# Two half-height passes in place of two full ones at the end of each projection

## The chip, the cores and the metric

The kernel runs on one core of a Trainium2 chip. The metric is the device time of one execution in microseconds (us). The kernel before has a median of 625.88 us over three runs (625.6 to 626.61). Engine names are those of the profile: PE is TensorE doing matmuls, PEld is TensorE loading the stationary operand ("weight load"), DVE is VectorE, ACT is ScalarE, POOL is GpSimd, SP is the queue that issues the transfers.

## The reference

Two linear-attention blocks read the same x (2048 rows of 576 numbers, 32 heads of 18) and are mixed by a gate that is computed from x:

```python
qkv = x @ wqkv                                  # A and B have weights of their own
# A: phi(t) = where(t > 0, t + 1, exp(t)) + 1e-6
# B: phi(t) = [softmax(t @ w_phi), softmax(-(t @ w_phi))]
kv  = einsum("bhsd,bhse->bhde", phi(k), v);  z = phi(k).sum(over s)
o   = einsum("bhqd,bhde->bhqe", phi(q), kv) / (einsum("bhqd,bhd->bhq", phi(q), z) + 1e-6)
a, b = oA @ woA, oB @ woB
g   = sigmoid((x * gate_w).sum(-1))
out = g * a + (1 - g) * b
```

All arrays are float32.

## The kernel before

**Tiles.** x is cut into 16 tiles of 128 rows and arrives transposed, so that the 576 columns of x lie on the partitions: four k-tiles of 128 rows, and a fifth (index 4) for the 64 that are left, which the host stores twice, in rows 0 to 63 and again in rows 64 to 127.

**Split operands.** The matmuls run on a rounded type, so each operand is kept as a high part and the rest: `load_x` makes `xh` and `xl`, `load_w` (through `split`) and `fold_w` make a weight tile `W` with nine slots: slots 0 to 3 are the high parts of k-tiles 0 to 3, slots 5 to 8 their low parts. Slot 4 is the tail: since the tail's rows stand twice, it holds the high part in rows 0 to 63 and the low part in rows 64 to 127.

**A projection** is x times one weight matrix, 576 columns (578 with the gate's two), in two column halves of `HB` = 288, each into a PSUM bank of its own. `proj` does one half in 14 passes of TensorE: for each of the four full k-tiles high x high, high x low, low x high; then `xh` with slot 4, which does the tail's high x high and high x low in one pass; then `xl` with slot 4. In this last pass only rows 0 to 63 give something that is wanted (low x high); rows 64 to 127 multiply low by low. There are 6 weight matrices and 16 tiles of x, so 96 projections and 192 halves: 2688 passes, all on line 157.

**The stages.** In the first, `do_v` makes the values (two halves, each in a one-bank PSUM tile `tr`, of which there are two), `do_ak` and `do_bk` the keys (`do_pq`: one two-bank tile `pq`, of which there are two), and `kv_a` and `kv_b` (line 212) add a tile's products to two PSUM banks `bk` that stay open for the whole stage. These last matmuls have 57 or 38 columns of stationary operand and write to PSUM partitions from 0 or from 64 on, in turn. Between the stages the sums are folded into the output weights; there line 351 writes 64 PSUM partitions at a time in the same manner. In the second stage `q_units` makes the queries of one tile (projections with `WBq` and `WAq`, into `pq`), `tr_units` transposes the features of the tile before, `num` and `out_units` finish an earlier one.

**Order.** The order of each engine's instructions is fixed when the program is built: a list scheduler follows the order of the code, the buffers and its own timing model, and may put matmuls of one group between those of another.

Of the kernel before, what the change touches and what calls it, by code (L numbers as in the profile page):

```python
# [10 lines left out]
AF = mybir.ActivationFunctionType  # L11
ALU = mybir.AluOpType
AX = mybir.AxisListType

P = 128
S, D, H, DH = 2048, 576, 32, 18
NT = S // P
KT = 5
HB = 288
# [9 lines left out]
def tile_gated_mix(ctx, tc, xT, wAk, wAv, wBv, wAq, wkT, wqT, phi, woA, woB, out):  # L29
    nc = tc.nc  # L30
    V, A, G, PE = nc.vector, nc.scalar, nc.gpsimd, nc.tensor
# [7 lines left out]
    def r(ap):  # L39
        return ap.bitcast(F32)  # L40

    def pq_tile():
        return ps.tile([P, 2, 512], F32, name="pq")

    def tr_tile():
        return ps.tile([P, 512], F32, name="tr")
# [4 lines left out]
    def row_tile():  # L51
        return wk.tile([P, 640], F32, name="row", bufs=6)

    def wraw_tile():
        return wk.tile([P, 640], F32, name="wraw", bufs=3)

    def uw_tile():
        return wk.tile([P, 2, D], F32, name="uw", bufs=3)
# [39 lines left out]
    def load_x(t, eng=G):  # L98
        raw = wk.tile([P, 640], F32, name="xraw")
        nc.sync.dma_start(raw, xT[t].rearrange("p j n -> p (j n)"))  # L100
        raw = raw.rearrange("p (j n) -> p j n", n=P)
        xh = wk.tile([P, KT, P], F32R, name="xh")
        xl = wk.tile([P, KT, P], F32R, name="xl")
        A.activation(xh, raw, AF.Copy)  # L104
        eng.tensor_tensor(xl, raw, r(xh), op=ALU.subtract)  # L105
        return xh, xl


    def w_tile():
        return wp.tile([P, 9, 578], F32R, name="W")  # L110

    def split(src, hi, lo, eng=V, raw=None):
        raw = (wraw_tile() if raw is None else raw)[:src.shape[0], :src.shape[1]]
        nc.sync.dma_start(raw, src)
        A.activation(hi, raw, AF.Copy)  # L115
        a = P - lo.shape[0] if hi.shape[0] == P else 0
        eng.tensor_tensor(lo, raw[a:], r(hi[a:]), op=ALU.subtract)

    def load_w(src, n, eng=V, raws=(None,) * KT):
        W = w_tile()  # L120
        for j in range(4):
            split(src[:, j, :], W[:, j, :n], W[:, 5 + j, :n], eng, raws[j])
        split(src[:, 4, :], W[:, 4, :n], W[64:, 4, :n], eng, raws[4])
        return W

    def fold_w(src):
        W = w_tile()
        ph = row_tile()
        nc.sync.dma_start(ph[:126, :630], phi)
        for g, nh in GROUPS:  # L130
            n = nh * DH
            c = slice(126 * g, 126 * g + n)
            raw = wraw_tile()
            nc.sync.dma_start(raw[:n, :], src[:n, g, :])
            if g % 2:
                p1, p2 = tr_tile(), tr_tile()
            else:
                pq = pq_tile()
                p1, p2 = pq[:, 0], pq[:, 1]
            for i in range(KT):  # L140
                dst = p1[:, 126 * i:126 * i + n] if i < 4 else p2[:, :n]
                PE.matmul(dst, raw[:n, P * i:P * i + P], ph[:n, 126 * g:126 * g + n], start=True, stop=True)  # L142
            p1v = p1[:, :504].rearrange("p (i c) -> p i c", c=126)[:, :, :n]
            A.activation(W[:, 0:4, c], p1v, AF.Copy)
            A.activation(W[:, 4, c], p2[:, :n], AF.Copy)
            V.tensor_tensor(W[:, 5:9, c], p1v, r(W[:, 0:4, c]), op=ALU.subtract)
            V.tensor_tensor(W[64:, 4, c], p2[64:, :n], r(W[64:, 4, c]), op=ALU.subtract)
        return W

    def proj(dst, x, W, c0, n):  # L150
        xh, xl = x
        steps = []
        for j in range(4):
            steps += [(xh, j, j), (xh, j, 5 + j), (xl, j, j)]
        steps += [(xh, 4, 4), (xl, 4, 4)]
        for i, (xx, j, w) in enumerate(steps):
            PE.matmul(dst, xx[:, j, :], W[:, w, c0:c0 + n], start=(i == 0), stop=(i == len(steps) - 1))  # L157

    def halves(p):
        return p[:, :, :HB]  # L160
# [1 line left out]
    def heads(p):  # L162
        return p[:, :, :HB].rearrange("p a (h d) -> p a h d", d=DH)

    def bc2(t):
        return t.rearrange("p (a h) -> p a h", a=2)[:, :, :, None].to_broadcast([P, 2, 16, DH])


    def phi_elu(pq):
        f = row_tile()  # L170
        fx = f[:, :D]
        fv = fx.rearrange("p (a b) -> p a b", a=2)
        A.activation(fv, halves(pq), AF.Exp)  # L173
        V.tensor_scalar(fx, fx, 1.0, EPS, op0=ALU.min, op1=ALU.add)  # L174
        V.scalar_tensor_tensor(fv, halves(pq), 1.0 + EPS, fv, op0=ALU.add, op1=ALU.max)  # L175
        return f

    def softmax_exp(pq):
        mm = sm.tile([P, 64], F32, name="mm")
        V.tensor_reduce(mm[:, :32], heads(pq), op=ALU.max, axis=AX.X)  # L180
        V.tensor_reduce(mm[:, 32:], heads(pq), op=ALU.min, axis=AX.X)
        uw = uw_tile()

        def v4(s):
            return uw[:, s, :].rearrange("p (a h d) -> p a h d", a=2, d=DH)

        V.tensor_tensor(v4(0), heads(pq), bc2(mm[:, :32]), op=ALU.subtract)
        V.tensor_tensor(v4(1), bc2(mm[:, 32:]), heads(pq), op=ALU.subtract)  # L188
        A.activation(uw, uw, AF.Exp)  # L189
        ss = sm.tile([P, 64], F32, name="ss")  # L190
        V.tensor_reduce(ss, uw.rearrange("p s (h d) -> p (s h) d", d=DH), op=ALU.add, axis=AX.X)  # L191
        rs = sm.tile([P, 64], F32, name="rs")
        V.reciprocal(rs, ss)  # L193
        return uw, rs
# [32 lines left out]
                     uw[:, :, 54 * gr:54 * gr + DH * nh], p == 1)  # L227

    def do_v(t, x, W, which):
        for hf in range(2):  # L230
            pv = tr_tile()
            proj(pv[:, :HB], x, W, HB * hf, HB)
            A.activation(vt[t % 2][:, which, 16 * hf:16 * hf + 16, :DH],  # L233
                         pv[:, :HB].rearrange("p (h d) -> p h d", d=DH), AF.Copy)

    def do_pq(x, W, n=D):
        pq = pq_tile()
        proj(pq[:, 0, :HB], x, W, 0, HB)
        proj(pq[:, 1, :n - HB], x, W, HB, n - HB)
        return pq  # L240

    def do_ak(x):
        return phi_elu(do_pq(x, WAk))
# [6 lines left out]
    xs = {0: load_x(0, V)}  # L250
    spare = [u[:, i] for u in (uw_tile(), uw_tile(), uw_tile()) for i in range(2)]
    WAv = load_w(wAv, D, raws=[None, None, None] + spare[:2])
    xs[1] = load_x(1)
    do_v(0, xs[0], WAv, 0)
    do_v(1, xs[1], WAv, 0)
    WAk = load_w(wAk, D, raws=spare[2:] + [None])
    f0 = do_ak(xs[0])
    f1 = do_ak(xs[1])
# [11 lines left out]
    for t in range(2, NT - 2):  # L270
        x = xs.pop(t)
# [9 lines left out]
        if t == 3:  # L281
            WBq = fold_w(wqT)
# [15 lines left out]
    WAq = load_w(wAq, 578, G)  # L298
# [8 lines left out]
    for p, kt in enumerate(kta):  # L307
        for a, m, n in widths(p):
            rows, c = slice(64 * a, 64 * a + m), P + 54 * a
            V.tensor_tensor(kt[rows, c:c + n], kv[0][rows, 54 * p:54 * p + n], mask[rows, a, :n], op=ALU.mult)  # L310
    for k in range(2):
        pz = tr_tile()
        w = min(324, D - 324 * k)
        for i in range(3):
            n = min(108, w - 108 * i)
# [8 lines left out]
    raw = wraw_tile()[:96, :D]  # L324
# [36 lines left out]
    def maps_a(pa):  # L361
        f = phi_elu(pa)
        gg = sm.tile([P, 2], F32, name="gg")
        for i, sgn in enumerate((-1.0, 1.0)):
            A.activation(gg[:, i:i + 1], pa[:, 1, HB:HB + 1], AF.Exp, scale=sgn)
        V.tensor_scalar(gg, gg, 1.0, None, op0=ALU.add)  # L366
        return f, gg

    def norm_a(f, gg):
        zw = row_tile()[:, :D]  # L370
        G.tensor_tensor(zw, f[:, :D], z_a, op=ALU.mult)  # L371
        den = sm.tile([P, 32], F32, name="den")
        V.tensor_reduce(den, zw.rearrange("p (h d) -> p h d", d=DH), op=ALU.add, axis=AX.X)  # L373
        V.tensor_scalar(den, den, EPS, gg[:, 0:1], op0=ALU.add, op1=ALU.mult)
        V.reciprocal(den, den)
        f3 = f[:, :D].rearrange("p (h d) -> p h d", d=DH)
        G.tensor_tensor(f3, f3, den[:, :, None].to_broadcast([P, 32, DH]), op=ALU.mult)
        A.activation(f[:, D:], f[:, 512:D], AF.Copy)
# [19 lines left out]
    def q_units(t, x=None):  # L398
        x = x or load_x(t)
        pb = pq_tile()  # L400
        proj(pb[:, 0, :HB], x, WBq, 0, HB)
        yield
        proj(pb[:, 1, :HB], x, WBq, HB, HB)
        sb = softmax_exp(pb)
        yield
        pa = pq_tile()
        proj(pa[:, 0, :HB], x, WAq, 0, HB)
        yield
        proj(pa[:, 1, :HB + 2], x, WAq, HB, HB + 2)
        sa = maps_a(pa)  # L410
        norm_a(*sa)
        qs[t] = (sa[0], sb[0])
        yield
        norm_b(*sb, sa[1])
# [93 lines left out]
    for p, kt in enumerate(ktb):  # L508
        b, o = b_region(p)
        for a, m, n in widths(p):  # L510
            rows, c = slice(64 * a, 64 * a + m), P + 54 * a
# [5 lines left out]
        n = min(108, D - 108 * p)  # L517
# [8 lines left out]
        g, nh = GROUPS[p - 1]  # L526
        n, w = nh * DH, (nh * DH if g < 4 else 80)
# [103 lines left out]
```

## Time and profile before

| | |
|---|---|
| median of three runs | 625.88 us |
| the profiled execution | 623.18 us |
| its span, first to last instruction | 621.5 us |
| PE busy | 604.0 us, 97% |
| PEld busy | 591.5 us, 95% |
| DVE, ACT, POOL busy | 391.5, 204.7, 174.4 us |
| granted TensorE clock | 1.0 of full speed |

Busy time of an engine is the time in which at least one of its instructions is shown as running. A matmul's row is longer than the time that it keeps TensorE from the next one, because matmuls are pipelined and their ends are modelled. What a pass costs is therefore read from the distance between the starts of successive rows.

### The profile page before, as it was taken

The numbers are of one execution on the slowest core, as the hardware profiler recorded it, in microseconds if no ns is written. First come the engines' busy times: TensorE is split into PE (matmuls) and PEld (weight loads), VectorE is DVE, ScalarE is ACT, GpSimd is POOL, SyncE is SP. The second block draws the span as 40 slices with busy tenths as digits, with TensorE's granted clock in tenths as the row PEclk, the third lists the DMA queues.
The fourth block names the chain that finished last, engine by engine and source line by source line (L and its number), as shares of the span: only waits on it lengthen the run. The fifth ranks groups of instructions, "written<-read, shape, count | busy, mean of one in ns | idle before, by whom it ended". The sixth has DMA issues, their size and how long they took to land.

```text
span 621.5 us, 11676 instructions
## 1 busy us (share of the span) xinstructions
PE 604.0 (97%) x5000; PEld 591.5 (95%) x5000; DVE 391.5 (63%) x644; ACT 204.7 (33%) x420; POOL 174.4 (28%) x126
## 2 busy tenths in 40 slices
PE   6999999999999999999998799999999999999997
PEld 6999999999999999999997599999999999999997
DVE  6373353323323332326999998989889988889920
ACT  6342232221222222235333344243332334332331
POOL 6013221112222222245245212434133443312300
PEclk9999999999999999999999999999999999999999
DMA  8441130000000000024011101011010110000001
GB/s 285 124 142 41 44 112 3 21 22 22 22 22 24 22 22 24 22 64 122 22 38 50 35 22 40 22 42 41 20 41 22 41 42 20 20 20 20 16 24 39
DMA packets 12660, 27.94 MB, mean 45 GB/s; under 512 B 1388, under 2 KB 1388, under 8 KB 12608
## 3 DMA queue, kind: packets, MB, share of 16 engines
q1 hardware_dynamic: 12608, 27.19, 14.1%
q8 instruction: 39, 0.64, 0.4%
q14 instruction: 13, 0.11, 0.1%
HBM read 22.47 MB, written 4.72 MB: 44 GB/s over the span
## 4 chain that ended last, share of the span: by engine, by line
PE 82%; DVE 13%; ACT 2%; DMA 2%; issue 1%; SPq 0%; ACTq 0%
PE pq L157 32%; PE tr L157 19%; PE bk L490 16%; PE bk L212 5%; PE tr L460 4%; PE tr L435 2%; DVE row L384 1%; DVE dd L385 1%; DMA wraw<-wBv 1%; DVE uw L198 1%; PE tr L428 1%; DVE W L424 1%; PE pq L142 1%; DVE gg L366 1%; DVE row L175 1%; DVE den L373 1%
## 5 line engine op out<-in xcount | busy, mean ns | idle before, releaser
L157 PE MATMUL pq<-W,xh 128*128 128x288 f32 (+1 forms) x1152 | 254.3, 300 | 0.2 <-DVE den L390 0.2
L157 PEld LDWEIGHTS pq<-W,xh 128*128 128x128 f32 x1152 | 190.9, 189 | 3.1 <-PE tr L348 0.6
L157 PE MATMUL pq<-W,xl 128*128 128x288 f32 (+1 forms) x640 | 187.1, 298 | 0.0
L157 PE MATMUL tr<-W,xh 128*128 128x288 f32 x576 | 124.4, 301 | 5.8 <-ACT W L115 5.3
L105 POOL TENSOR_TENSOR xl<-xraw,xh 128x640 fp32r<-128x640 f32 x29 | 45.4, 1566 | 301.2 <-ACT xh L104 300.6
L157 PEld LDWEIGHTS pq<-W,xl 128*128 128x128 f32 x640 | 120.8, 189 | 0.2
L157 PEld LDWEIGHTS tr<-W,xh 128*128 128x128 f32 x576 | 96.7, 193 | 6.6 <-ACT W L115 5.3
L157 PE MATMUL tr<-W,xl 128*128 128x288 f32 x320 | 93.9, 299 | 0.0
L174 DVE TENSOR_SCALAR row<-row 128x576 f32<-128x576 f32 x32 | 24.4, 762 | 101.2 <-ACT row L173 101.2
L233 ACT ACTIVATE vo<-tr 128x288 f32<-128x288 f32 x64 | 25.9, 407 | 150.2 <-PE tr L157 150.2
L490 PE MATMUL bk<-W,ath 128*128 128x288 f32 x288 | 63.5, 301 | 1.1 <-ACT ath L423 0.7
L191 DVE TENSOR_REDUCE ss<-uw 128x64 f32<-128x1152 f32 x32 | 43.2, 1351 | 31.0 <-ACT uw L189 30.9
L157 PEld LDWEIGHTS tr<-W,xl 128*128 128x128 f32 x320 | 61.8, 193 | 0.0
L490 PE MATMUL bk<-W,vo 126*128 126x288 f32 x384 | 61.3, 299 | 0.0
L490 PEld LDWEIGHTS bk<-W,vo 126*128 126x128 f32 x384 | 54.0, 189 | 0.0
L180 DVE TENSOR_REDUCE mm<-pq 128x32 f32<-128x576 f32 x32 | 23.9, 748 | 47.0 <-PE pq L157 47.0
L189 ACT ACTIVATE uw<-uw 128x1152 f32<-128x1152 f32 x32 | 37.3, 1167 | 41.7 <-DVE uw L188 41.0
L490 PEld LDWEIGHTS bk<-W,ath 128*128 128x128 f32 x288 | 47.2, 189 | 1.5 <-ACT ath L423 0.9
L490 PE MATMUL bk<-W,atl 128*128 128x288 f32 x160 | 47.4, 297 | 0.0
L371 POOL TENSOR_TENSOR row<-row,z_a 128x576 f32<-128x576 f32 x16 | 30.1, 1882 | 52.5 <-DVE row L175 52.5
L460 PE MATMUL tr<-W,kb_h 126*126 126x256 f32 (+1 forms) x160 | 32.4, 283 | 1.0 <-DVE vo L465 0.8
L198 POOL TENSOR_TENSOR uw<-uw,rs 128x1152 f32<-128x1152 f32 x15 | 32.3, 2155 | 0.7 <-DVE rs L193 0.7
(138 smaller groups left out, 875.7 us busy)
## 6 DMA issues: line engine op xcount, KB each, us to landing
xraw<-xT SPq DMA_DIRECT2D x30, 320.0 KB, 3.1
out<-row SPq DMA_DIRECT2D x16, 288.0 KB, 2.1
wraw<-woA SPq DMA_DIRECT2D x6, 288.0 KB, 2.9
wraw<-wAq SPq DMA_DIRECT2D x5, 289.0 KB
wraw<-wBv SPq DMA_DIRECT2D x5, 288.0 KB, 4.2
wraw<-wkT SPq DMA_DIRECT2D x4, 315.0 KB
wraw<-wqT SPq DMA_DIRECT2D x4, 315.0 KB
uw<-wAk SPq DMA_DIRECT2D x4, 288.0 KB
```

The lines of the kernel that those rows point to most:

```text
L105: eng.tensor_tensor(xl, raw, r(xh), op=ALU.subtract)
L157: PE.matmul(dst, xx[:, j, :], W[:, w, c0:c0 + n], start=(i == 0), stop=(i == len(steps) - 1))
L174: V.tensor_scalar(fx, fx, 1.0, EPS, op0=ALU.min, op1=ALU.add)
L180: V.tensor_reduce(mm[:, :32], heads(pq), op=ALU.max, axis=AX.X)
L189: A.activation(uw, uw, AF.Exp)
L191: V.tensor_reduce(ss, uw.rearrange("p s (h d) -> p (s h) d", d=DH), op=ALU.add, axis=AX.X)
L198: eng.tensor_tensor(u3, u3, rs[:, :, None].to_broadcast([P, 64, DH]), op=ALU.mult)
L212: PE.matmul(dst, vt[t % 2][:, which, 3 * gr:3 * gr + nh, :].rearrange("p h d -> p (h d)"), rhs, start=(t == 0 and first), stop=(t == NT - ...
L233: A.activation(vt[t % 2][:, which, 16 * hf:16 * hf + 16, :DH], pv[:, :HB].rearrange("p (h d) -> p h d", d=DH), AF.Copy)
L371: G.tensor_tensor(zw, f[:, :D], z_a, op=ALU.mult)
L460: PE.matmul(dst, kk[:n, i, :w], uu[:n, i, :256], start=(m == 0), stop=(m == 5))
L490: PE.matmul(po[:, :HB], l, w, start=(i == 0), stop=(i == len(steps) - 1))
```

## The change

Slot 4 of `W` is arranged anew: for the first 288 columns it holds the high part in rows 0 to 63 and the low part in rows 64 to 127, as before; for the other columns the low part is in rows 0 to 63 and the high part in rows 64 to 127. `xh` with slot 4 still gives both products in one pass. `proj` now has 13 passes for a half and leaves the group open. The last pass of both halves moves to the new `proj_tail`: two matmuls of 64 rows each, one on rows 0 to 63 for the first half of the columns, one on rows 64 to 127 for the second, each into its half's bank. The number of matmuls stays the same. `do_v` now takes both of its `tr` tiles first, projects both halves, runs the two tails and then copies both halves out. Building the low part of slot 4 takes two DVE (or POOL) instructions where the 288th column lies inside a block, else one.

```diff
+    def tail_low(W, c0, c1, src, eng):
+        for rows, b0, b1 in ((slice(64, P), c0, min(c1, HB)), (slice(0, 64), max(c0, HB), c1)):
+            if b0 < b1:
+                w = W[rows, 4, b0:b1]
+                eng.tensor_tensor(w, src[rows, b0 - c0:b1 - c0], r(w), op=ALU.subtract)
...
-            V.tensor_tensor(W[64:, 4, c], p2[64:, :n], r(W[64:, 4, c]), op=ALU.subtract)
+            tail_low(W, 126 * g, 126 * g + n, p2, V)
...
-        steps += [(xh, 4, 4), (xl, 4, 4)]
-        for i, (xx, j, w) in enumerate(steps):
-            PE.matmul(dst, xx[:, j, :], W[:, w, c0:c0 + n], start=(i == 0), stop=(i == len(steps) - 1))
+        for i, (xx, j, w) in enumerate(steps + [(xh, 4, 4)]):
+            PE.matmul(dst, xx[:, j, :], W[:, w, c0:c0 + n], start=(i == 0), stop=False)
+
+    def proj_tail(d0, d1, x, W, n=HB):
+        for a, dst in enumerate((d0, d1)):
+            rows = slice(64 * a, 64 * a + 64)
+            PE.matmul(dst, x[1][rows, 4, :], W[rows, 4, HB * a:HB * a + (n if a else HB)], start=False, stop=True)
...
     def do_v(t, x, W, which):
+        pv = [tr_tile()[:, :HB] for _ in range(2)]
         for hf in range(2):
-            pv = tr_tile()
-            proj(pv[:, :HB], x, W, HB * hf, HB)
+            proj(pv[hf], x, W, HB * hf, HB)
+        proj_tail(*pv, x, W)
+        for hf in range(2):
             A.activation(vt[t % 2][:, which, 16 * hf:16 * hf + 16, :DH],
-                         pv[:, :HB].rearrange("p (h d) -> p h d", d=DH), AF.Copy)
+                         pv[hf].rearrange("p (h d) -> p h d", d=DH), AF.Copy)
```

`do_pq` and `q_units` call `proj_tail` in the same way after their second half.

**What moves on TensorE, first stage.** The rows below are TensorE's instructions in one turn of the first stage before, where a key projection of A (`W_204` is its weight tile) is followed by the products of the tile before it (`bk`) and then by the key projection of B. A row names line, operation, output and inputs; `x2` means twice in a row.

```order
L157 MATMUL pq_1310<-W_204,xh_1178 128x288 x2
L157 MATMUL pq_1310<-W_204,xl_1179 128x288
L157 MATMUL pq_1310<-W_204,xh_1178 128x288
L157 MATMUL pq_1310<-W_204,xl_1179 128x288
L212 MATMUL bk_104<-row_1172,vo_102 57x54 x10
L212 MATMUL bk_104<-row_1172,vo_102 38x36
L212 MATMUL bk_104<-uw_1236,vo_102 57x108 x2
L212 MATMUL bk_105<-uw_1236,vo_102 57x108 x8
L212 MATMUL bk_105<-uw_1236,vo_102 38x72
L157 MATMUL pq_1371<-W_298,xh_1178 128x288 x2
```

The same turn in the changed program, in two pieces. First the end of the key projection of A (line 166 is a full pass, line 171 a tail):

```order
L166 MATMUL pq_1315<-W_205,xh_1183 128x288 x2
L166 MATMUL pq_1315<-W_205,xl_1184 128x288
L166 MATMUL pq_1315<-W_205,xh_1183 128x288
L171 MATMUL pq_1315<-W_205,xl_1184 128x288 x2
L226 MATMUL bk_104<-row_1177,vo_102 57x54 x3
L166 MATMUL tr_1283<-W_115,xh_1183 128x288 x2
```

Then, 26 full passes of a value projection later:

```order
L166 MATMUL tr_1284<-W_115,xl_1184 128x288
L166 MATMUL tr_1284<-W_115,xh_1183 128x288
L171 MATMUL tr_1283<-W_115,xl_1184 128x288
L171 MATMUL tr_1284<-W_115,xl_1184 128x288
L226 MATMUL bk_104<-row_1177,vo_102 57x54 x7
L226 MATMUL bk_104<-row_1177,vo_102 38x36
L226 MATMUL bk_104<-uw_1241,vo_102 57x108 x2
L226 MATMUL bk_105<-uw_1241,vo_102 57x108 x8
L226 MATMUL bk_105<-uw_1241,vo_102 38x72
L166 MATMUL pq_1376<-W_300,xh_1183 128x288 x2
```

The two tails stand next to each other, and the 22 matmuls on `bk` that were one block are now two, of 3 and of 19, each behind a pair of tails.

**What moves on TensorE, at the start.** The end of the first value projection before, whose two halves are mixed:

```order
L157 MATMUL tr_140<-W_115,xh_108 128x288
L157 MATMUL tr_140<-W_115,xl_109 128x288
L157 MATMUL tr_156<-W_115,xh_108 128x288
L157 MATMUL tr_156<-W_115,xl_109 128x288
L157 MATMUL pq_221<-W_204,xh_108 128x288
```

and in the changed program:

```order
L166 MATMUL tr_141<-W_115,xh_108 128x288
L171 MATMUL tr_141<-W_115,xl_109 128x288
L166 MATMUL tr_142<-W_115,xh_108 128x288
L171 MATMUL tr_142<-W_115,xl_109 128x288
L166 MATMUL pq_223<-W_205,xh_108 128x288
```

Here a full pass stands between the two tails. Over the whole program 89 of the 96 pairs of tails stand next to each other, and 7 pairs (14 tails) stand apart. Matmuls on 64 PSUM partitions (`bk`, and the block of line 351) form 23 blocks before and 35 after; 27 of the 35 come directly behind a tail.

More of the change, by code (lines that the diff above doesn't have):

```diff
@@ L115, in split @@
         A.activation(hi, raw, AF.Copy)
-        a = P - lo.shape[0] if hi.shape[0] == P else 0
-        eng.tensor_tensor(lo, raw[a:], r(hi[a:]), op=ALU.subtract)
+        eng.tensor_tensor(lo, raw, r(hi), op=ALU.subtract)
+    def tail_low(W, c0, c1, src, eng):
[3 more added lines that the diff above has]
+                eng.tensor_tensor(w, src[rows, b0 - c0:b1 - c0], r(w), op=ALU.subtract)
     def load_w(src, n, eng=V, raws=(None,) * KT):
@@ L122, in load_w @@
             split(src[:, j, :], W[:, j, :n], W[:, 5 + j, :n], eng, raws[j])
-        split(src[:, 4, :], W[:, 4, :n], W[64:, 4, :n], eng, raws[4])
+        raw = (wraw_tile() if raws[4] is None else raws[4])[:, :n]
+        nc.sync.dma_start(raw, src[:, 4, :])
+        A.activation(W[:, 4, :n], raw, AF.Copy)
+        tail_low(W, 0, n, raw, eng)
         return W
@@ L229, in do_v, with do_pq @@
     def do_v(t, x, W, which):
+        pv = [tr_tile()[:, :HB] for _ in range(2)]
         for hf in range(2):
-            pv = tr_tile()
-            proj(pv[:, :HB], x, W, HB * hf, HB)
+            proj(pv[hf], x, W, HB * hf, HB)
+        proj_tail(*pv, x, W)
+        for hf in range(2):
             A.activation(vt[t % 2][:, which, 16 * hf:16 * hf + 16, :DH],
-                         pv[:, :HB].rearrange("p (h d) -> p h d", d=DH), AF.Copy)
-    def do_pq(x, W, n=D):
+                         pv[hf].rearrange("p (h d) -> p h d", d=DH), AF.Copy)
+    def do_pq(x, W):
         pq = pq_tile()
         proj(pq[:, 0, :HB], x, W, 0, HB)
-        proj(pq[:, 1, :n - HB], x, W, HB, n - HB)
+        proj(pq[:, 1, :HB], x, W, HB, HB)
+        proj_tail(pq[:, 0, :HB], pq[:, 1, :HB], x, W)
         return pq
@@ L403, in q_units @@
         proj(pb[:, 1, :HB], x, WBq, HB, HB)
+        proj_tail(pb[:, 0, :HB], pb[:, 1, :HB], x, WBq)
         sb = softmax_exp(pb)
@@ L409, in q_units @@
         proj(pa[:, 1, :HB + 2], x, WAq, HB, HB + 2)
+        proj_tail(pa[:, 0, :HB], pa[:, 1, :HB + 2], x, WAq, HB + 2)
         sa = maps_a(pa)
```

## The prediction

> **What bounds the kernel now.** I read the page first: busy shares, the forty slices, the chain that ended last, the costliest groups.
>
> ```profile
> span 621.5 us, 11676 instructions
> PE 604.0 (97%) x5000; PEld 591.5 (95%) x5000; DVE 391.5 (63%) x644; ACT 204.7 (33%) x420; POOL 174.4 (28%) x126
> ...
> PEclk9999999999999999999999999999999999999999
> ...
> PE 82%; DVE 13%; ACT 2%; DMA 2%; issue 1%; SPq 0%; ACTq 0%
> ...
> L157 PE MATMUL pq<-W,xh 128*128 128x288 f32 (+1 forms) x1152 | 254.3, 300 | 0.2 <-DVE den L390 0.2
> ...
> L157 PE MATMUL pq<-W,xl 128*128 128x288 f32 (+1 forms) x640 | 187.1, 298 | 0.0
> L157 PE MATMUL tr<-W,xh 128*128 128x288 f32 x576 | 124.4, 301 | 5.8 <-ACT W L115 5.3
> ...
> L157 PE MATMUL tr<-W,xl 128*128 128x288 f32 x320 | 93.9, 299 | 0.0
> ...
> L233 ACT ACTIVATE vo<-tr 128x288 f32<-128x288 f32 x64 | 25.9, 407 | 150.2 <-PE tr L157 150.2
> ```
>
> TensorE carries the kernel: 82% of the last chain, at full clock. The projections are 1152 + 640 + 576 + 320 = 2688 of its 5000 matmuls, and next to nothing of its idle time stands ahead of them. A busy share cannot say whether TensorE also has slack inside, so I looked at busy time by stage (all engines, then line 157 alone) and at the chain in order of time.
>
> ```profile
> core 0: us, PE busy (x) PEld busy (x) DVE busy (x) ACT busy (x) POOL busy (x), PEclk, DMA share, GB/s
> 43.00:305.00 262.00, 261.91 (x2395) 256.80 (x2396) 104.01 (x155) 72.88 (x131) 68.40 (x40) 1.00 0.12 36
> 305.00:357.00 52.00, 45.51 (x323) 40.62 (x322) 49.72 (x94) 18.14 (x47) 21.34 (x14) 1.00 0.15 43
> 357.00:621.00 264.00, 259.51 (x1997) 258.04 (x1995) 214.05 (x360) 93.19 (x208) 74.16 (x47) 1.00 0.09 29
> ```
>
> ```profile
> 305.00:357.00 52.00, 29.38 (x189) 26.00 (x189) 1.00 0.15 43
> ```
>
> ```profile
> 131.26 3.94 PE pq L157 x28
> 135.19 3.71 PE tr L157 x28
> ...
> 146.38 1.80 PE bk L212 x43
> 148.18 3.94 PE pq L157 x28
> ```
>
> The stage up to 305 us has no gap on TensorE, the one after 357 us hardly any. Only between them, where DVE is busy for 49.7 of 52 us, does TensorE wait (6.5 us). A pass in steady flow takes 3.71 / 28 = 0.133 us; one turn of the first stage takes 148.18 - 131.26 = 16.92 us. So nearly every nanosecond that TensorE gains or loses reaches the end.
>
> **The change, part by part.** *Passes.* 192 full passes go and 192 half-height ones come, in 96 pairs. Where the two of a pair run side by side, a pair takes one pass's time: 89 pairs stand next to each other in the program's order, and each saves 0.133 us, 11.8 us in all. The 14 tails that stand apart save nothing.
>
> *Switching.* No matmul of the kernel before works on 64 rows, so the price of going to half height and back has to be bounded. The nearest rows on the cheap side are those in the output stage where the number of rows changes from 128 to 80, 72 and back:
>
> ```profile
> 385.05 0.30 PE L490 MATMUL bk<-W,atl 128*128 128x288 f32 x1
> 385.19 0.30 PE L490 MATMUL bk<-wob_x,vo 80*128 80x288 f32 x1
> 385.32 0.30 PE L490 MATMUL bk<-wob_y,vo 72*128 72x288 f32 x1
> 385.46 0.30 PE L157 MATMUL pq<-W,xh 128*128 128x288 f32 x1
> ```
>
> The starts are 0.13 to 0.14 us apart, as ever: fewer rows alone cost nothing. But these still use the array as one piece. The rows in which it is cut in two, by columns, are line 351 (64 of 128 columns in turn) and line 212. First the way in, with TensorE's rows and then the weight loads:
>
> ```profile
> 350.91 0.30 PE L157 MATMUL pq<-W,xl 128*128 128x288 f32 x1
> 351.05 0.29 PE L157 MATMUL pq<-W,xh 128*128 128x288 f32 x1
> 351.27 2.16 PE L351 MATMUL tr<-wraw,atl 128*64 128x288 f32 x16
> ```
>
> ```profile
> 350.91 0.19 PEld L157 LDWEIGHTS pq<-W,xh 128*128 128x128 f32 x1
> 351.27 0.13 PEld L351 LDWEIGHTS tr<-wraw,atl 128*64 128x64 f32 x1 [0.16 <-issue]
> ```
>
> ```profile
> 146.09 0.29 PE L157 MATMUL pq<-W,xl 128*128 128x288 f32 x1
> 146.31 0.26 PE L212 MATMUL bk<-row,vo 128*57 128x54 f32 x1
> ```
>
> In ordinary flow a weight load starts with the matmul before its own (350.91 in both lists), 0.13 us ahead. At the cut it starts 0.22 us after the last full matmul and together with its own matmul's row: 0.09 us of waiting, in both places, and then the load itself is no longer hidden. The way out, with the last two of line 351:
>
> ```profile
> 353.02 0.41 PE L351 MATMUL tr<-wraw,atl 128*64 128x288 f32 x2
> 353.36 0.40 PE L157 MATMUL pq<-W,xh 128*128 128x288 f32 x1
> 353.60 0.30 PE L157 MATMUL pq<-W,xl 128*128 128x288 f32 x1
> ```
>
> ```profile
> 353.36 0.19 PEld L157 LDWEIGHTS pq<-W,xh 128*128 128x128 f32 x1 [0.44 <-issue]
> 353.47 0.19 PEld L157 LDWEIGHTS pq<-W,xl 128*128 128x128 f32 x1
> ```
>
> The sixteen matmuls of line 351 run as eight pairs: 2.16 - 0.41 = 1.75 us for seven distances between pairs and the first unhidden load, 0.24 us a pair and 0.05 us for that load. That two halves do run side by side is seen from full matmuls of the same type and length, which take (0.89 - 0.41) / 2 = 0.24 us each:
>
> ```profile
> 328.49 0.89 PE L348 MATMUL tr<-wraw,ath 128*128 128x288 f32 x3
> ```
>
> Going out, 353.36 - 353.02 = 0.34 us less the pair's own 0.24 is 0.10 us of waiting; then the full weights show: 0.24 us to the second matmul where 0.13 is usual, and 0.11 us between the two loads. So a switch costs 0.09 to 0.10 us of waiting plus the first load, 0.11 us for 128 columns, 0.05 for 57 or 64: about 0.20 us into half height (its weights have 128 columns) or back to full, 0.14 us into the column blocks.
>
> Between the ends, nothing and 0.20 us each way, I take 0.20: half height by rows cuts the array in two as line 351 does, and the 72 and 80 rows do not.
>
> [...]
>
> *The sum.* In the changed order there are 103 entries into half height (89 pairs, 14 single tails): 20.6 us. 76 of them lead back to full passes: 15.2 us. 27 lead into a block on `bk`: 27 x 0.14 = 3.8 us. Those blocks are now 35 instead of 23, 8 of them entered from full passes instead of 23: 12 x 0.20 - 15 x 0.14 = +0.3 us. Together 39.9 us, less the 11.8 us of passes: +28.1 us, or +0.27 us for each pair (0.20 + 0.20 - 0.13) and more for the single tails.
>
> *What is hidden.* In the stretch from 305 to 357 us the 189 projection matmuls are some 7 pairs; 7 x 0.27 = 1.9 us go into TensorE's 6.5 us of waiting there. If that cover were gone, DVE would have to be faster. Net +26.2 us.
>
> *The rest, at nothing.* `do_v` holds both `tr` tiles to the end and copies them out afterwards, 2 x 0.41 = 0.8 us on ACT; in the steady turn 26 full passes, 3.5 us, stand ahead of the next use of `tr`, so TensorE need not wait. At the start only 8 passes, 1.1 us, stand there, which is close. The additional instructions for slot 4 run on DVE, which is busy for 104 of the 262 us up to 305. No transfer changes.
>
> The profiled execution took 623.18 us, 2.7 us under the median of the runs. Its time becomes 649.4 us; on the median, which I predict, 625.9 + 26.2 = 652 us.
>
> **The rivals.** *Half height is entered for nothing*, like the 72 and 80 rows (the faster side). Then 11.8 us go, and 12 more column blocks at 0.14 + 0.20 cost 4.1: -7.7 us, 618 us. For it speaks only that the number of rows is free in line 490. It decides from a price under 7.7 / 103 = 0.075 us for in and out together; line 351 pays 0.09 of waiting for the way in alone.
>
> [...]
>
> *The array waits, but the weights still load ahead.* Entry 0.09, way back 0.10, blocks as before: 103 x 0.09 + 76 x 0.10 + 3.8 + 0.3 = 21.0 us, less 11.8: +9.2 us, less 0.4 hidden: about 635 us. Against it: both lists of weight loads show the load starting only after the wait.
>
> *The tails of a pair do not run side by side* (the change does not do what it says). Without a price for switching, only the 4.1 us of blocks are left: 630 us. With the full price, 652 + 11.8 = 664 us. Against it: line 351's pairs, though these are columns.
>
> **How the numbers follow.** Chances: 0.64 for the full price, 0.12 for the wait alone, 0.15 for switching at nothing, 0.05 for tails in turn without a price, 0.04 with it. The predicted time is that of the first, 652 us; its own range is 645 to 660, for waits at the start, where the cover is short, and for a price that differs by some hundredths of a microsecond each way. The range for 8 in 10 takes in the two cases just below it: 629 to 662 us. What this kernel's measurement can tell from no change is about 0.2%, 1.3 us. Faster by more: 0.15, the one rival; within: 0.03; slower by more: 0.82.
>
> **What would show it.** After a full pass, the first row of line 171 should start 0.22 us later with its weight load beside it, the second less than 0.01 us behind it, the next full pass 0.34 us later (0.11 of load, 0.13 of its own, 0.10 of waiting) and the one after that another 0.24 us later. The turn of 16.92 us has, in the new order, four entries, two returns, two ways into blocks and two out of them: 0.8 + 0.4 + 0.28 + 0.4 = 1.88 us, less 0.34 for the old block and 4 x 0.133 for the passes: 17.9 us. Switching at nothing would give 16.7 us, the wait alone 17.3, tails in turn at full price 18.5. I am wrong if the starts around line 171 stay 0.13 us apart.

## The result and the profile after

The changed kernel takes 645.11 us (median of four runs, 644.56 to 646.15), against 626.25 us before (625.6 to 627.23): ratio 1.030, 95% interval 1.028 to 1.032, 18.9 us slower. I had forecast slower, 652 us, range 629 to 662. The page of the profile, busy shares, granted clock, chain and the two groups of `proj` into `pq`:

```profile
span 642.8 us, 11679 instructions
PE 627.6 (98%) x5000; PEld 587.2 (91%) x5000; DVE 390.4 (61%) x649; ACT 202.1 (31%) x420; POOL 172.6 (27%) x127
...
PEclk9999999999999999999999899999999999999999
...
PE 91%; DVE 6%; DMA 2%; ACT 1%; issue 0%; ACTq 0%
...
L166 PE MATMUL pq<-W,xh 128*128 128x288 f32 (+1 forms) x1152 | 245.9, 303 | 0.8 <-ACT gg L382 0.8
...
L166 PE MATMUL pq<-W,xl 128*128 128x288 f32 (+1 forms) x512 | 152.3, 297 | 0.0
```

TensorE is even more the bound, 91% of the chain. Its busy time grew by 23.6 us with the same 5000 matmuls, while that of its weight loads fell. The page does not tell why; the starts of single rows do. One pair of tails in the first stage, first the matmuls, then the weight loads:

```profile
143.67 0.30 PE L166 MATMUL pq<-W,xl 128*128 128x288 f32 x1
143.80 0.29 PE L166 MATMUL pq<-W,xh 128*128 128x288 f32 x1
144.03 0.40 PE L171 MATMUL pq<-W,xl 64*128 64x288 f32 x2
144.35 0.54 PE L166 MATMUL tr<-W,xh 128*128 128x288 f32 x2
```

```profile
143.67 0.19 PEld L166 LDWEIGHTS pq<-W,xh 128*128 128x128 f32 x1
144.02 0.19 PEld L171 LDWEIGHTS pq<-W,xl 64*128 64x128 f32 x2 [0.16 <-issue]
144.35 0.30 PEld L166 LDWEIGHTS tr<-W,xh 128*128 128x128 f32 x2
```

The full pass starts 0.13 us after the one ahead of it, the pair 0.22 us after that, with its loads beside it and not ahead of it; two matmuls fit into one row of 0.40 us, so they do run side by side. The next full pass starts 0.32 us behind them, again together with its load. Counted over all 89 pairs of the trace, the medians are 0.225 us in (from the start of the last full pass), 0.003 us between the two, 0.326 us out (from the second tail to the next start), and 0.237 us to the second full pass where full passes follow. The chain in order of time gives one turn of the first stage:

```profile
140.46 3.63 PE pq L166 x26
144.42 3.65 PE tr L166 x26
...
156.69 1.59 PE bk L226 x37
158.29 3.63 PE pq L166 x26
```

It takes 158.29 - 140.46 = 17.83 us, 16.92 before.

### The profile page after: what moved, and what is told of

Its sections match the earlier page's. It is cut to its first block, busy times and chain, and to the rows that moved or that the text cites. A ratio compares the mean times of both kernels' runs of the same rounds, so it can differ in the third digit from the quotient of the medians.

```text
span 642.8 us, 11679 instructions
## 1 busy us (share of the span) xinstructions
PE 627.6 (98%) x5000; PEld 587.2 (91%) x5000; DVE 390.4 (61%) x649; ACT 202.1 (31%) x420; POOL 172.6 (27%) x127
## 4 chain that ended last, share of the span: by engine, by line
PE 91%; DVE 6%; DMA 2%; ACT 1%; issue 0%; ACTq 0%
PE pq L166 33%; PE bk L509 19%; PE tr L166 19%; PE bk L226 5%; PE tr L479 4%; PE pq L171 3%; PE tr L454 2%; PE tr L171 2%; PE tr L447 1%; PE pq L152 1%; DVE dd L402 1%; DVE uw L212 1%; DMA wraw<-wqT 1%; DVE row L401 1%; DMA xraw<-xT 0%; DMA wraw<-wkT 0%
## 5 line engine op out<-in xcount | busy, mean ns | idle before, releaser
L166 PE MATMUL pq<-W,xh 128*128 128x288 f32 (+1 forms) x1152 | 245.9, 303 | 0.8 <-ACT gg L382 0.8
L166 PEld LDWEIGHTS pq<-W,xh 128*128 128x128 f32 x1152 | 186.0, 189 | 6.8 <-ACT gg L382 1.3
L166 PE MATMUL pq<-W,xl 128*128 128x288 f32 (+1 forms) x512 | 152.3, 297 | 0.0
L166 PEld LDWEIGHTS tr<-W,xh 128*128 128x128 f32 x576 | 94.0, 192 | 9.1 <-ACT W L117 5.4
L166 PEld LDWEIGHTS pq<-W,xl 128*128 128x128 f32 x512 | 96.7, 189 | 1.0 <-issue 0.4
L166 PE MATMUL tr<-W,xl 128*128 128x288 f32 x256 | 76.2, 298 | 0.0
L166 PEld LDWEIGHTS tr<-W,xl 128*128 128x128 f32 x256 | 49.3, 193 | 0.0
L249 ACT ACTIVATE vo<-tr 128x288 f32<-128x288 f32 x64 | 23.0, 404 | 61.4 <-PE tr L171 61.4
L187 ACT ACTIVATE row<-pq 128x576 f32<-128x576 f32 x32 | 20.6, 645 | 43.2 <-PE pq L171 43.2
L442 ACT ACTIVATE W<-tr 126x512 fp32r<-126x512 f32 (+1 forms) x44 | 23.2, 527 | 30.8 <-DVE atl L463 17.2
```

Source lines behind the costliest of these rows:

```text
L442: A.activation(h, src, AF.Copy)
```

## Experiments

Theory: each entry of the array into half height and each return costs waiting and a weight load that nothing hides. Rivals: the order that came with the edit costs the time (tails behind both halves, both `tr` tiles held, blocks on `bk` split); or a tail as such is slow, or the pairs don't overlap.

| run | median us | its before | ratio, 95% interval |
|---|---|---|---|
| full-height tails, moved | 627.13 | 626.43 | 1.0008 (0.9988 to 1.0027) |
| 64 rows, not moved | 689.07 | 626.43 | 1.100 (1.098 to 1.102) |
| 72 rows, not moved | 626.64 | 626.43 | 1.0005 (0.9995 to 1.0016) |
| both tails on rows 0 to 63 | 655.28 | 626.43 | 1.046 (1.044 to 1.047) |
| blocks of four tails | 639.51 | 626.06 | 1.022 (1.020 to 1.024) |
| half height in the first stage only | 638.58 | 626.06 | 1.021 (1.019 to 1.023) |
| half height for the queries only | 632.75 | 626.06 | 1.011 (1.009 to 1.013) |
| `bk` products of two tiles together | 624.07 | 626.06 | 0.9971 (0.9959 to 0.9982) |
| query tails moved, full height | 624.59 | 626.27 | 0.9973 (0.9960 to 0.9987) |
| the last two together | 622.37 | 626.27 | 0.9939 (0.9926 to 0.9952) |

**Everything moved, nothing cut.**

```diff
-            rows = slice(64 * a, 64 * a + 64)
+            rows = slice(0, P)
```

> The changed program with its tails on all 128 rows (low by low comes back in, as before), moved code and order kept: 35 blocks on the kv banks instead of 23, no half height. If the price lies in switching the array to half height and back: before plus at most 12 blocks x 0.34 us = 4.1 us, 626 to 630 us, and the full pass behind the tail follows at 0.13 us. If the price lies in what was moved (tails behind both halves, both tr tiles held, kv blocks split): about 645 us, like the changed kernel.

627.13 us: without half height the changed kernel takes the time of the kernel before. The price lies in half height, 645.11 - 627.13 = 18.0 us. In this trace the order did cost and gain something in places, which is told below.

**64 rows against 72, nothing moved.** In the kernel before, only the last pass of each half is shortened (its low by low product falls away in part or whole):

```diff
-            PE.matmul(dst, xx[:, j, :], W[:, w, c0:c0 + n], ...)
+            rows = slice(0, 64) if i == len(steps) - 1 else slice(0, P)    # or slice(0, 72)
+            PE.matmul(dst, xx[rows, j, :], W[rows, w, c0:c0 + n], ...)
```

> The kernel before, with the last pass of each half on rows 0 to 63 alone; nothing moved, no pairs: 192 entries into half height instead of the changed kernel's 103. If each entry and each return costs some 0.20 us: 192 x 0.20 + 176 x 0.20 = 73.6 us more than before, some of it hidden, 690 to 700 us. If a tail matmul as such is slow, whatever surrounds it: 192 tails as in the changed kernel, about 645 us. If moving the tails was the price: 626 us.

> The same edit with 72 rows instead of 64, the only difference to the kernel with rows 0 to 63. If the price is that of cutting the array in two, 72 rows don't fit a half and nothing changes: 626 us, starts 0.13 us apart. If fewer rows as such cost something: near the kernel with 64 rows.

With 64 rows the kernel takes 689.07 us, with 72 rows 626.64. TensorE's rows around one such pass, of the kernel with 64 rows and then of the one with 72:

```profile
150.87 0.29 PE L158 MATMUL pq<-W,xh 128*128 128x288 f32 x1
151.10 0.39 PE L158 MATMUL pq<-W,xl 64*128 64x288 f32 x1
151.42 0.53 PE L158 MATMUL pq<-W,xh 128*128 128x288 f32 x2
```

```profile
151.03 0.29 PE L158 MATMUL pq<-W,xh 128*128 128x288 f32 x1
151.16 0.29 PE L158 MATMUL pq<-W,xl 72*128 72x288 f32 x1
151.30 0.29 PE L158 MATMUL pq<-W,xh 128*128 128x288 f32 x1
```

The starts are 0.23 and 0.32 us apart with 64 rows, 0.13 and 0.14 with 72. Eight rows less cost 62 us over the kernel. The step from 72 rows to 64 carries the price, not a short pass as such nor its place. 62 us is below the 73.6 us worked out. Row for row against the kernel with 72 rows, the 192 tails cost 68.0 us, each counted to the second start behind it: 0.38 us each in the median where full passes follow, 0.20 where a block on `bk` does. The other 5.6 us went into TensorE's waits.

**Do the two of a pair run side by side?** Both tails on the same rows (slot 4 arranged as before):

```diff
-            rows = slice(64 * a, 64 * a + 64)
+            rows = slice(0, 64)
```

> The changed program with both tails of a pair on rows 0 to 63 (slot 4 arranged as before): same number of entries, but the two cannot run side by side. If the pairs of the changed kernel do run side by side: 89 x 0.13 us more for the second stream, 657 us, and up to 668 us if its weight load is not hidden either. If they already run one after the other in the changed kernel: 645 us.

655.28 us, 10.2 more than the changed kernel, 0.114 us for each of 89 pairs. TensorE's rows and loads:

```profile
152.83 0.29 PE L166 MATMUL tr<-W,xh 128*128 128x288 f32 x1
153.05 0.53 PE L171 MATMUL tr<-W,xl 64*128 64x288 f32 x2
153.51 0.54 PE L166 MATMUL pq<-W,xh 128*128 128x288 f32 x2
```

```profile
153.05 0.29 PEld L171 LDWEIGHTS tr<-W,xl 64*128 64x128 f32 x2 [0.16 <-issue]
153.51 0.30 PEld L166 LDWEIGHTS pq<-W,xh 128*128 128x128 f32 x2 [0.16 <-issue]
```

From the first tail to the next full pass it is now 0.46 us, 0.32 before: one more stream, whose load was hidden behind the first. So in the changed kernel the two overlap wholly. The change did what it says, and lost.

**Is the price by switch or by tail?** In the main loop a key and a value projection are both left open and their four tails issued together:

```diff
+        for hf in range(2):
+            proj(pq[:, hf, :HB], x, Wk, HB * hf, HB)
+        for hf in range(2):
+            proj(pv[hf], x, Wv, HB * hf, HB)
+        proj_tail(pq[:, 0, :HB], pq[:, 1, :HB], x, Wk)
+        proj_tail(*pv, x, Wv)
```

> The changed program with the tails of a key and a value projection put together in the main loop of the first stage: blocks of four tails, 78 entries into half height instead of 103, 192 tails as before. If the price is by switch: 8.5 us less than the changed kernel, 637 us; 639 us if the second pair's weight load is not hidden. If it is by tail matmul or by pair: 645 us, no change.

639.51 us: 5.6 us less with the same 192 tails and 25 entries fewer. That is near the upper of the two values given, but not for its reason. The loads of a block of four, and the same value projection in two successive turns of the chain:

```profile
154.10 0.18 PEld L171 LDWEIGHTS pq<-W,xl 64*128 64x128 f32 x2 [0.17 <-issue]
154.21 0.19 PEld L171 LDWEIGHTS tr<-W,xl 64*128 64x128 f32 x2
```

```profile
133.49 3.46 PE tr L166 x26
...
150.71 3.46 PE tr L166 x26
```

The second pair's loads start 0.11 us after the first pair's and run beside its stream, so they are hidden. The turn takes 17.22 us, 0.61 less than in the changed kernel; over the 12 turns of the main loop that would be 7.3 us. The other 1.7 I put down to the clock. In this trace TensorE's granted clock (the column before the last two) falls to half for 3.41 us of the first stage, with TensorE busy throughout:

```profile
93.73:97.14 3.41, 3.41 (x17) 3.41 (x16) 1.46 (x4) 0.91 (x4) 2.03 (x1) 0.50 0.64 162
```

Half of 3.41 us, 1.7 us, is my estimate of what this stretch took, and the changed kernel's trace is at full clock there. The mean clock of this kernel's four runs is 0.992 to 0.994, that of the changed kernel's 0.994 to 0.997. The price is by switch.

**Where does it count?** Half height in one stage only, full-height tails in the other:

```diff
-            rows = slice(64 * a, 64 * a + 64)
+            rows = slice(64 * a, 64 * a + 64) if half else slice(0, P)
```

> The changed program with half-height tails in the first stage only (64 projections), full-height tails for the 32 query projections. By the traces of before and after, the first stage gave 18.6 of the 21.4 us, so about 642 us, and the stretch after it should take as long as before. If the whole price of 0.27 us a pair counts everywhere: 645 less 34 x 0.27 = 636 us.

> The complement: half-height tails in the query projections only. If waits for DVE take up part of the price there: 626 plus 4 for the kv blocks plus 3, 631 to 634 us. If all of the price counts: 626 + 4 + 9.6 = 640 us.

638.58 and 632.75 us. Against the fully moved kernel without half height these are 11.5 and 5.6 us; together 17.1, near the 18.0 of both. The first run is 3 us under what I expected: I had read the first stage's whole growth as half height's and taken the rest as before, but the moved order, which this run keeps, gave 2.6 us back in the output stage. The second lies within 631 to 634, but not because waits took up part of the price. In the table below the queries' half height costs the output stage 5.8 us, and the 2.6 us of the order stand against it. The stages can be read from the first and last starts of the matmuls on `bk` (operation by line; durations as least, median and most in ns, then first and last start). Before, after, and with full-height tails:

```profile
L212 PE MATMUL bk<-uw,vo x352: 225/255/302, 50.3 to 299.9; 128*57 128x108 f32 x160, 128*38 128x72 f32 x16
L490 PE MATMUL bk<-W,ath x288: 289/296/402, 355.9 to 615.7; 128*128 128x288 f32 x144
L490 PE MATMUL bk<-wob_y,vo x32: 291/300/382, 375.3 to 617.7; 72*128 72x288 f32 x32
```

```profile
L226 PE MATMUL bk<-uw,vo x352: 224/255/302, 53.6 to 318.5; 128*57 128x108 f32 x160, 128*38 128x72 f32 x16
L509 PE MATMUL bk<-W,ath x288: 289/297/403, 374.0 to 637.0; 128*128 128x288 f32 x144
L509 PE MATMUL bk<-wob_y,vo x32: 291/300/383, 393.8 to 639.0; 72*128 72x288 f32 x32
```

```profile
L226 PE MATMUL bk<-uw,vo x352: 225/255/302, 51.8 to 305.9; 128*57 128x108 f32 x160, 128*38 128x72 f32 x16
L509 PE MATMUL bk<-W,ath x288: 289/296/402, 362.4 to 619.6; 128*128 128x288 f32 x144
L509 PE MATMUL bk<-wob_y,vo x32: 291/299/382, 381.5 to 621.6; 72*128 72x288 f32 x32
```

| us | before | full-height tails, moved | half height in stage 1 | for the queries | after |
|---|---|---|---|---|---|
| first stage | 299.9 | 305.9 | 318.6 | 305.9 | 318.5 |
| between | 56.0 | 56.5 | 55.5 | 55.7 | 55.5 |
| output stage | 261.8 | 259.2 | 259.3 | 265.0 | 265.0 |

**Two versions that the price points to.** I estimated 0.34 us for a block of column-cut matmuls, 0.14 in and 0.20 out by the rows of before, so fewer blocks should gain. In the kernel before, the `bk` products wait for every second tile:

```diff
-        if pend[0] is not None:
-            kv_a(t - 1, pend[0])
-        kv_b(t - 1, pend[1])
+        if t % 2 == 0:
+            kv_all()              # both tiles that are waiting; a third buffer vt[2] lies in kts[3]
```

> The kernel before, with the kv products of two tiles issued together (a third buffer for the values, taken from a tile that is free then): 19 blocks on half of the columns instead of 23, nothing else. If a block costs 0.14 us in and 0.20 us out whatever its kind: 4 x 0.34 = 1.4 us less than before, ratio 0.998. If switching only costs around half-height rows: no change.

0.9971: 1.4 us expected, 2.0 measured. Two turns take 162.53 - 129.00 = 33.53 us by its chain, against 2 x 16.92 = 33.84 before:

```profile
129.00 3.46 PE bk L214 x86
...
162.53 3.46 PE bk L214 x86
```

The other came from the table: with full-height tails the output stage was 2.6 us shorter than before. So the query projections' last passes alone were moved, at full height:

```diff
-        steps += [(xh, 4, 4), (xl, 4, 4)]
+        steps += [(xh, 4, 4), (xl, 4, 4)][:2 if whole else 1]
...
+            PE.matmul(p[:, a, :m], x[1][:, 4, :], W[:, 4, HB * a:HB * a + m], start=False, stop=True)
```

> The kernel before with only the order of the query projections changed: both halves' last passes, full height, behind the second half. In the trace of the changed program with full-height tails the output stage took 2.6 us less than before (259.2 against 261.8 us from its first to its last output matmul). If moving the last passes is what removed waits there: 626 - 2.6 = 623.5 us, output stage about 259 us. If that stage was shorter for another reason, such as the schedule ahead of it: 626 us, no change.

> The kernel before with both edits that gained something alone: kv products of two tiles together (19 blocks instead of 23) and the query projections' last passes, full height, behind both halves. If the two are independent: 2.0 + 2.6 us less, 621.5 us, ratio 0.993. If the second is nothing: 624 us, as with the first edit alone.

1.7 us for the move alone (I expected 2.6; its output stage takes 260.8 us), 3.9 us for both, 622.37 us: the two add up, and this version beats both kernels. The longest wait of TensorE in the output stage before has no counterpart in the moved version:

```profile
582.79 0.34 PE L460 MATMUL tr<-W,kb_h 72*80 72x256 f32 x1 [0.75 <-DVE vo L465]
```

It is 0.75 us on a DVE subtraction. It accounts for a part of the gain only; what makes up the rest stays open.

## Why the prediction was right, and where its size was off

**The mechanism was right.** Row by row the price of column cuts held for row cuts, by the medians of after: in 0.09 us of waiting (0.225 - 0.133), from the tails to the next start 0.19 for the load that is not hidden and the waiting on the way out (0.326 - 0.133, where 0.21 was forecast), and 0.10 to the second full pass (0.237 - 0.133). A turn of 17.93 us was worked out (written as 17.9), 17.83 measured. Pairs do overlap (0.003 us apart). In the kernel before, shortening the last pass to 64 rows cost 62 us and shortening it to 72 rows nothing (689.07 and 626.64 us, 626.43 before). So the overlap inside a block came with a price for the way in and out, and that price decided here.

**The size was off by 7.3 us** (26.2 forecast, 18.9 measured), which put the time at the lower edge of the 645 to 660 us given for the full price. By terms:

- *The base.* The sum was made against a profiled execution and added to the median of the runs. Between the two profiled executions the difference is 21.4 us (644.56 - 623.18); between the medians 18.9. Before's profiled execution is 3.1 us below its own median, and its mean granted clock is 1.000, as in few runs. Between the stages TensorE waits for DVE; the timeline and the busy times of that stretch in the trace of after:

```profile
362.57 1.08 PE L454 MATMUL bk<-ident,uw 128*126 128x128 f32 x4 [2.67 <-DVE uw L212]
```

```profile
362.10:365.60 3.50, 3.03 (x10) 2.36 (x11) 3.47 (x11) 0.60 (x1) 0.94 (x1) 0.51 0.32 94
```

  Around the end of the wait of 2.67 us stand 3.5 us at a granted clock of 0.51. The trace of before has a longer wait at the same place, and full clock behind it:

```profile
344.74 0.52 PE L435 MATMUL bk<-ident,uw 128*126 128x128 f32 x3 [3.83 <-DVE uw L198]
```

```profile
344.74:348.24 3.50, 3.42 (x18) 2.50 (x19) 3.50 (x10) 1.95 (x7) 1.75 (x2) 1.00 0.00 1
```

  Three other runs of the kernel before at clock 1.0 took 623.8 to 624.4 us, those at 0.996 and 0.997 between 625.05 and 627.2. One stretch of 3.41 us at half clock takes 0.003 off the mean of 623 us, so by this estimate a clock of 0.997 fits one such stretch. Some 2 us of before's median go with the lower mean clock, and its profiled execution, at 1.000, has no such stretch; where one lies in before's other runs no trace shows.
- *"The rest, at nothing."* Full-height tails show what the move alone did by stage: +6.0 us in the first, where 4.1 us were forecast for the split blocks, and -2.6 us in the output stage, where nothing was. The first holds a wait for the last transfer of `fold_w` that I had not seen coming: 1.50 us with full-height tails and 1.97 in after, shown here, against 0.2 before. The kernel with 72 rows, which moved nothing, has 0.8 us of it, so not all of it need be the order's:

```profile
93.28 0.30 PE L152 MATMUL pq<-row,wraw 72*128 72x72 f32 x1 [1.97 <-DMA wraw<-wqT]
```

- *What is hidden.* 1.9 us forecast, all of it between the stages. There, half height left the time 1.0 us shorter than full-height tails (55.5 against 56.5 us) although 8 pairs lie in it (7 were counted on). Their price, some 2.1 us, was covered, mostly by waits on DVE. The 1.0 us more goes with the clock: the trace with full-height tails is at half clock for 6.83 us there, after for 3.41, before not at all:

```profile
348.59:355.42 6.83, 5.48 (x19) 3.30 (x19) 6.13 (x14) 1.29 (x3) 2.56 (x2) 0.50 0.17 48
```

  In the first stage half height cost 318.5 - 305.9 = 12.6 us; 32 pairs into full passes at 0.256, 27 into blocks at 0.07 and 12 single tails at 0.39 make 14.8, so 2.2 us were covered by waits there.
- *The price itself.* In the output stage 13 of 22 pairs are followed by transposes, whose second start comes 0.165 us after the first instead of 0.109, not 0.236 instead of 0.133: 0.21 us a pair, not 0.27. 13 x 0.21 + 9 x 0.256 + 0.7 for the split pair are 5.7 us; measured, 265.0 - 259.2 = 5.8. Over all stages the rows give 14.8 + 2.1 + 5.7 = 22.6 us for half height alone, where the sum had 28.1 - 4.1 = 24.0.

Together: 2.5 us by the base, 2.6 - 1.9 = 0.7 by the order, 2.2 + 3.1 - 1.9 = 3.4 by what was hidden, 1.4 by the price, less 0.5 us by which the stretch between the stages was longer with full-height tails than before (there too the clocks differ): 7.5, near the 7.3 that were off. The terms come from one trace of each kernel, so single tenths mean little.

The rivals: switching at nothing (0.15) and the wait alone (0.12) fall by the rows with 64 rows, tails in turn by the run on the same rows.

## What to carry to other kernels

Count the switches between shapes and price them from rows of a trace, not the rows or columns saved: here a single pass of 64 rows between full passes cost 0.38 us more in the median than one of 72 rows, which takes 0.13 as a full pass does, and a pair of them 0.256 us more than two full passes (0.092 + 0.193 + 0.104 - 0.133, from the medians of after). So on these prices half height could pay only in longer blocks. By these rows a further pair in a block saves 0.13 us, one stream in place of two passes, and three pairs in one block would about break even (0.256 - 2 x 0.133 us; an estimate, since no run here had more than two). A shape that is in the trace already, here by columns, gave the price of one that was not, to within 0.02 us.

## What the runs showed of the hardware

The step between 72 and 64 rows: nothing (626.64 us, 626.43 before) against 0.38 us a pass in the median where full passes follow. And a stretch of 3.41 us at half clock (0.50 granted) that comes and goes. In after it starts during a wait of TensorE of 2.67 us (0.50 from 362.2 us on, the wait ends at 362.57), and in the kernel with blocks of four tails one stands from 93.73 us on, behind a wait of 2.0 us; none stands at the wait of 3.83 us in before or at that of 1.97 us in the first stage of after, so the length of the wait alone does not decide. What does was not shown. Of the runs of the kernel before, those at a mean clock of 1.0 took 623.2 to 624.4 us, those at 0.996 and 0.997 between 625.05 and 627.2. A base taken from one profiled execution should be set against the clock of the other runs first.
